# An S4 convolution beside a feed-forward block: where the first half's sums wait, and how the convolution's last step joins them

## The chip, the cores and the metric

The kernel runs on one core of one Trainium2 chip. Its time is the device time of one execution in microseconds (us), from the first to the last of the program's work. The runs before the change took 1136.37 us in the median of three (1135.81 to 1136.94).

Five engines of the core appear in the texts: PE (TensorE, the matrix multiplier), ACT (ScalarE), DVE (VectorE), POOL (GpSimd) and SP (SyncE, which here issues DMAs only). Each engine works through its own list of instructions in order. An instruction waits until the semaphores that it names allow it to go, and what stands behind it on the same engine waits with it. DMAs are issued by an instruction of SP, ACT or POOL and then run on the core's 16 DMA engines.

## What is computed

For 2048 tokens of width 576 the reference gives the sum of three terms: the input itself, a state-space convolution (S4, 128 states per channel, done by FFT) of the normalised input, and a feed-forward block with SiLU of the same normalised input.

```python
x = A_u                                   # (1, 2048, 576)
xn = _layernorm(x)
# _A_ref: K[d, l] = Re sum_n C dt B exp(dt A l);  y = irfft(rfft(xn) * rfft(K))[:L] + xn * Dskip
# _B_ref: silu(xn @ w1) @ w2,  w1 (576, 4608), w2 (4608, 576)
return x + _A_ref(xn, ...) + _B_ref(xn, w1, w2)
```

## The kernel before

All data is float32. For accuracy each matrix operand is split into a rounded part and a rest (`gh` and `gl`, `w1h` and `w1l`, the two planes of `w`), and a product is three matmuls of the parts. ACT makes the rounded part by a cast, DVE the rest by a subtraction.

**Tokens.** The 2048 tokens are 16 groups of 128, numbered j = 0 to 15; "token j" in the texts means such a group. Groups 0 to 7 are the first half, 8 to 15 the second. Each half is two blocks of four groups (b = 0, 1). An accumulator `acc[j]` of 128x576 in SBUF begins as x and takes up the feed-forward sum; two groups share one tile (`pairs`), and the pool `accp` has four such tiles, so the eight accumulators of one half fill it.

**Feed-forward.** `ffn` goes through the hidden width in chunks c of 4 x 128. For each (half, chunk, block) `up` multiplies by w1 (L289 to L291), applies SiLU on ACT (L297), and splits the result into `gh` (L298) and `gl` (L299); `down` multiplies by w2 into two PSUM banks `po` (L318) and DVE adds them to `acc[j]` (L323). The weights are loaded on SP into `w1r` (L244 to L246) and `w2r` (L266) and split (`w1h` on ACT L361, `w1l` on DVE L362 in the later part; `w` on ACT L275 and DVE L277). Split w2 tiles of the first half are kept in the scratch `dw2` and loaded again on POOL in the second (`w<-dw`, L471). From the third chunk of the second half on, `wino_ffn` does the products with w1 in a form with seven instead of eight block products (L444, L450, with sums of quarters on DVE, L372 to L375, and combinations `f`, L519).

**Between the halves.** At the first half's last chunk, when group j is complete, `down` stores `acc[j]` to a scratch in device memory, `dr0` (L326, on SP, shown as `dr<-acc`). After an odd j it loads x for groups 7+j and 8+j into a new tile of `accp` (L328 calls `load_x`, whose four DMAs are at L166, on SP).

**Convolution.** `side` is a second generator that `weave` steps through at positions (0 to 1) between the steps of `ffn`. It normalises x, transposes it (`spread`, L139 to L158, with loads `xr` on SP, stores `d1u<-u` on POOL), builds the kernel's spectrum (`kgen`, DVE and ACT work at L776 to L883), multiplies spectra (`spectral`, L889 to L942) and leaves d2 in device memory (`d<-yo`). What is left is the last step: a multiplication by a small matrix `s4`, by `conv` (L1005), with 64x32 tiles of the matrix multiplier, eight matmuls per group into two PSUM banks. Its operands `ys` are loaded on SP by `conv_load` (L993, two DMAs of 288 KB per group, six groups ahead).

**Tail.** `tail`, the last part of `side`, does that step for groups 0 to 7. `load_r0` loads two stored sums from `dr0` (L953, one DMA of 576 KB on SP, shown as `r<-dr`); `last` does `conv` for one group into two banks of the pool `pss` and DVE adds these to the loaded sums (`add_conv`, L1016); after the second group of a pair `store` writes the pair to the output with four DMAs on POOL (L173, `out_dram<-r`). The positions are in `tail_at`. For groups 8 to 15 the step is done in `down` at the second half's last chunk: `conv` writes two groups into four banks (`begun`; L1005, shown as `po`), and the feed-forward matmuls add to the same banks.

PSUM has eight banks in three pools: `ps1` (2 banks: `ph`, `pa`, `pc`), `ps2` (3 banks: `po`, `pb`) and `pss` (3 banks, used by `side`). The pair that `begun` holds lies in ps2 (first group) and ps1 (second group).

**Order.** The order of the instructions on each engine is not that of the program text: a scheduler that simulates the timeline places them, led by priorities (`tc.high_priority`) and by pinned dependences (`behind`).

Of the kernel before, what the change touches and what calls it, by code (L numbers as in the profile page):

```python
# [10 lines left out]
F32 = mybir.dt.float32  # L11
F32R = mybir.dt.float32r
AF = mybir.ActivationFunctionType
ALU = mybir.AluOpType
# [3 lines left out]
P = 128  # L18
L = 2048
D = 576  # L20
# [4 lines left out]
HD = D // 2  # L25
# [16 lines left out]
def kernel(  # L42
# [21 lines left out]
    nc = tc.nc  # L64
# [13 lines left out]
    dram = ctx.enter_context(tc.tile_pool(name="dram", bufs=1, space=DRAM))  # L78
# [2 lines left out]
    d2 = dram.tile([32 * P, D], F32, name="d2")  # L81
    dxt = [dram.tile([P, 9, 512], F32, name=f"dxt{b}") for b in range(2)]
    dxn = dram.tile([P, NJ, D], F32, name="dxn")
    dr0 = dram.tile([8 * P, D], F32, name="dr0")
    dw2 = dram.tile([NFT - WINO_C * FT, P, 2, D], F32, name="dw2")
    dexp = dram.tile([P, 4 * D], F32, name="dexp")

# [15 lines left out]
    accp = ctx.enter_context(tc.tile_pool(name="accp", bufs=4))  # L103
# [3 lines left out]
    ps1 = ctx.enter_context(tc.tile_pool(name="ps1", bufs=2, space=PSUM))  # L107
    ps2 = ctx.enter_context(tc.tile_pool(name="ps2", bufs=3, space=PSUM))
    pss = ctx.enter_context(tc.tile_pool(name="pss", bufs=3, space=PSUM))

    acc = {}
# [20 lines left out]
    pairs = {}  # L132
# [29 lines left out]
    def load_x(j, pool, tag, engines):  # L162

        t = pool.tile([P, 2, D], F32, tag=tag, name=f"{tag}{j}")
        for ps, v, eng in quarters(xv, engines):
            eng.dma_start(t[ps], v[:, j:j + 2])  # L166
        pairs[j] = t
        return t[:, 0, :], t[:, 1, :]

    def store(t, j, engines):  # L170

        for ps, v, eng in quarters(ov, engines):
            eng.dma_start(v[:, j:j + 2] if len(t.shape) > 2 else v[:, j], t[ps])  # L173

    def norm(p0, js, xs):

# [52 lines left out]
    def ffn():  # L229
# [71 lines left out]
        def down(blk, jj, terms=None):  # L301
            half, c, b = blk
            j = 8 * half + 4 * b + jj
            js = slice(jj * P, (jj + 1) * P)
            if half == 1 and c == NCH - 1 and jj % 2 == 0:
                for i, (pool, tag) in enumerate(((ps2, "ps2"), (ps1, "ps1"))):
                    begun[j + i] = [pool.tile([P, 512], F32, tag=tag, name="po") for _ in range(2)]
                conv((j, j + 1), (begun[j], begun[j + 1]))
                for i in range(2):
                    conv_load(j + i + AHEAD)  # L310
            terms = terms or [(G[blk, t], W2[half, c, t]) for t in range(FT)]
            for h in range(2):
                hs = slice(h * HD, (h + 1) * HD)
                po = begun[j][h] if j in begun else ps2.tile([P, 512], F32, tag="ps2", name="po")
                n = 0
                for gs, ws in terms:
                    for g, w in ((0, 0), (0, 1), (1, 0)):
                        pins["pe"] = nc.tensor.matmul(po[:, :HD], gs[g][:, js], ws[:, w, hs],  # L318
                                                      start=n == 0 and j not in begun, stop=n == 3 * len(terms) - 1,
                                                      skip_group_check=j in begun).ins  # L320
                        n += 1
                with tc.high_priority():
                    nc.vector.tensor_add(acc[j][:, hs], po[:, :HD], acc[j][:, hs])  # L323
            if half == 0 and c == NCH - 1:
                rows = slice(j * P, (j + 1) * P)
                nc.sync.dma_start(dr0[rows, :], acc[j])  # L326
                if j % 2:
                    acc[7 + j], acc[8 + j] = load_x(7 + j, accp, "acc", (nc.sync,))  # L328

        def next_xt(b):  # L330
            xt = new_xt(2 + b)
# [614 lines left out]

    def tail():

        r0s = {}

        def load_r0(j):
            r0s[j] = yp.tile([P, 2, D], F32, tag="r0", name="r0", bufs=2)
            nc.sync.dma_start(r0s[j], dr0[j * P:(j + 2) * P, :].rearrange("(i p) d -> p i d", p=P))  # L953

        def last(j):
            add_conv(j, r0s[j - j % 2][:, j % 2, :])
            conv_load(j + AHEAD)
            if j % 2:
                store(r0s[j - 1], j - 1, (nc.gpsimd,))

        steps, at = [], tail_at[0]
        for j in range(8):
            for f in (conv_load, load_r0)[j >= AHEAD:2 - j % 2]:
                steps.append((at, f, j))
                at += tail_at[1]
        steps += [(tail_at[2] + j * tail_at[3], last, j) for j in range(8)]
        for at, f, j in sorted(steps, key=lambda v: v[0]):
            yield at
            with behind(pins["load"]):
                f(j)  # L970
# [18 lines left out]
    def conv_load(j):  # L989
        if j < NJ:  # L990
            yss[j] = yp.tile([P, 4, HD], F32, tag="ys", name="ys", bufs=AHEAD)
            for h in range(2):
                nc.sync.dma_start(yss[j][64 * h:64 * h + 64],  # L993
                                  d2[j * 256:(j + 1) * 256, h * HD:(h + 1) * HD].rearrange("(q r) d -> r q d", q=4))

    def conv(js, banks):

        ys = [yss.pop(j) for j in js]
        first = pins["pe"]
        for n in range(8 * len(js)):  # L1000
            i, q1, q2, h = n // 8, n // 4 % 2, n // 2 % 2, 1 - n % 2
            o = 64 * q1 + 32 * q2
            rows = slice(64 * h, 64 * h + 64)
            with tc.high_priority() if n else nullcontext(), behind(first):
                mm = nc.tensor.matmul(banks[i][h][o:o + 32, :HD], s4[rows], ys[i][rows, 2 * q2 + q1],  # L1005
                                      start=True, stop=True, tile_position=(64 * h, o), skip_group_check=True)
            if n == 0:
                first = mm.ins

    def add_conv(j, dst):  # L1010

        py = [pss.tile([P, 512], F32, tag="pss", name="py") for _ in range(2)]
        conv((j,), (py,))
        for h in range(2):
            hs = slice(h * HD, (h + 1) * HD)
            nc.vector.tensor_add(dst[:, hs], py[h][:, :HD], dst[:, hs])  # L1016

    def gate_of(i):

        return (FT + i * 2 * FT + 1) / (2 * NCH * 2 * 2 * FT)  # L1020
# [1 line left out]
    def side():  # L1022
        nonlocal s4, kl, yp, pa, kfp, tail_at
        marks = (0.1357, 0.613, 0.855)
        tail_at = (0.893, 0.003, 0.930, 0.005)
        with tc.tile_pool(name="pa", bufs=4) as pa:
            for js in ((0, 1), (2, 3), (4, 5), (6, 7)):
                with behind(pins["xt3"] if js[0] > 2 else None):
                    phase0(pa, js)
                pins[f"xt{js[1]}"], pins[f"xt{js[1]}s"] = pins["xt_v"], pins["xt_s"]  # L1030
                if js[0] == 2:
                    yield 0
            yield 0
        with tc.tile_pool(name="kf", bufs=1) as kfp:
            for n in ("f", "rho", "phi"):
                kf[n] = kfp.tile([P, D], F32, name=n + "T")
            with tc.tile_pool(name="nat", bufs=1) as nat, tc.tile_pool(name="pb", bufs=2) as pb:
                nt = natural(nat)
                tiles = iter(range(8, NJ, 2))
                for at, tables in ((0.0, 1), (0.02, 0), (0.035, 0), (gate_of(1), 1), (0.06, 0), (gate_of(2), 1), (0.08, 0), (0.085, 1)):  # L1040
                    yield at
                    if tables:
                        next(nt, None)
                    else:
                        j = next(tiles)
                        with behind(pins["gl"]):
                            phase0(pb, (j, j + 1))
            with behind(pins["sd"]):
                nc.gpsimd.dma_start(f1, cf1)
            nc.sync.dma_start(vt, cv)  # L1050
            with tc.tile_pool(name="up", bufs=1) as up:
                sp = spread(up)
                for n, at in enumerate(kgen()):
                    if n > 1:
                        next(sp, None)
                    yield marks[0] + at * (marks[1] - marks[0])
                for _ in sp:
                    pass
        s4p = ctx.enter_context(tc.tile_pool(name="s4p", bufs=1))
        s4 = s4p.tile([P, 32], F32, name="s4")  # L1060
        nc.gpsimd.dma_start(s4, cs4)

        xp = ctx.enter_context(tc.tile_pool(name="xp", bufs=1))
        with tc.tile_pool(name="sx", bufs=1) as sx:
            for k, _ in enumerate(wino_x(sx, xp)):
                yield (171 + k) / 276
        with tc.tile_pool(name="kl", bufs=1) as kl:
            for at in spectral():
                yield 176 / 276 + (at - 1) * (marks[2] - 176 / 276)
        yp = ctx.enter_context(tc.tile_pool(name="yp", bufs=3))  # L1070
        yield from tail()
# [89 lines left out]
```

## Time and profile before

| | |
|---|---|
| median of three runs | 1136.37 us (1135.81 to 1136.94) |
| the profiled execution | 1141.59 us |
| its span (first to last instruction) | 1139.8 us |
| mean granted clock of PE | 0.990 |
| busy: PE, DVE, ACT, POOL | 1104.0, 955.5, 721.1, 113.4 us |
| moved by DMA | 176.04 MB, mean 154 GB/s |

The profile shows one execution. Times are in us from the start of the span unless marked ns. A timeline row gives the start, the duration, engine, line of the kernel's text, operation, destination<-source, the tile shape, and the count of equal instructions put together; in brackets the idle time before it and what released the engine. PE's float32 matmuls appear as several records each. "SPq" rows are the issuing of DMAs by SP; their duration includes waiting between the DMAs of one group, and the time to landing is told elsewhere. A row of the waits gives the waiting engine and line, what it waited for, the sum, the count and the longest. The table of stretches gives, for each stretch of time, the busy time and count for each engine, the granted clock of PE (PEclk, 1.00 is full), the busy share of the DMA engines and their rate.

### The profile page before, as it was taken

Reading aid. Unit: us, or ns where it says so; the run is one execution under the profiler, and the core shown is the slowest. Engines: PE = TensorE matmul, PEld = TensorE weight load, DVE = VectorE, ACT = ScalarE, POOL = GpSimd, SP = SyncE. Lnnn points to the kernel's source line nnn. Section 1 sums busy time; section 2 is a strip of 40 time slices with the busy share of each in tenths; the row PEclk is TensorE's granted clock in tenths of the full one; section 3 lists DMA queues with packets and bytes.
Section 4 is the critical chain, followed back from the end, with each engine's and each line's share of the span. In section 5 each row is a group of like instructions: output and inputs, shape, how many; then the busy total and the mean of one; then the engine's idle time right before and its main releaser. Section 6 shows DMA issues by size and latency. Waiting matters only on the chain.

```text
span 1139.8 us, 23099 instructions
## 1 busy us (share of the span) xinstructions
PE 1104.0 (97%) x9101; PEld 991.5 (87%) x9101; DVE 955.5 (84%) x1631; ACT 721.1 (63%) x1269; POOL 113.4 (10%) x206
## 2 busy tenths in 40 slices
PE   6999999999999999999989999999999999999798
PEld 5998989888988899899988889999989899998576
DVE  6698898999999999999979988988888888884432
ACT  4665456676677666676747646887867777772210
POOL 1001000000000000000000002112112112210111
PEclk9999999999999999999989999999999999999899
DMA  9456523536263625376844137556455556547964
GB/s 274 131 160 197 165 97 101 144 109 167 83 166 108 188 86 150 109 218 215 230 124 115 54 64 219 153 172 181 141 161 148 171 171 187 176 121 180 260 172 109
DMA packets 171405, 176.04 MB, mean 154 GB/s; under 512 B 88432, under 2 KB 136576, under 8 KB 170656
## 3 DMA queue, kind: packets, MB, share of 16 engines
q1 hardware_dynamic: 150128, 120.91, 38.4%
q0 software_dynamic: 20784, 52.76, 14.7%
q8 instruction: 72, 1.18, 0.4%
q10 hardware_dynamic: 384, 0.89, 0.3%
q14 instruction: 37, 0.30, 0.1%
HBM read 112.00 MB, written 62.60 MB: 153 GB/s over the span
## 4 chain that ended last, share of the span: by engine, by line
PE 52%; DVE 21%; DMA 10%; issue 7%; ACT 7%; SPq 1%; POOL 1%; DVEq 0%; ACTq 0%; POOLq 0%
PE po L318 23%; PE ph L289 12%; DMA w1r<-in_B_w_dram 5%; PE pb L444 3%; DVE acc L323 2%; PE kp L855 2%; PE pc L444 2%; DMA w2r<-in_B_w_dram 1%; DVE th L798 1%; DMA ys<-d 1%; DVE S L834 1%; DVE C L834 1%; PE pb L986 1%; PE pu L986 1%; DVE gl L299 1%
## 5 line engine op out<-in xcount | busy, mean ns | idle before, releaser
L318 PE MATMUL po<-w,gh 128*128 128x288 f32 x2304 | 479.5, 297 | 8.2 <-ACT gh L298 3.8
L318 PEld LDWEIGHTS po<-w,gh 128*128 128x128 f32 x2304 | 378.2, 189 | 26.7 <-issue 5.6
L318 PE MATMUL po<-w,gl 128*128 128x288 f32 x1152 | 337.3, 297 | 0.4 <-DVE gl L299 0.4
L318 PEld LDWEIGHTS po<-w,gl 128*128 128x128 f32 x1152 | 216.2, 189 | 3.9 <-issue 1.4
L323 DVE TENSOR_TENSOR acc<-po,acc 128x288 f32<-128x288 f32 x296 | 130.5, 451 | 61.9 <-PE po L318 60.6
L289 PE MATMUL ph<-xh,w1h 128*128 128x512 f32 (+1 forms) x368 | 99.7, 389 | 0.9 <-ACT xh L124 0.6
L289 PE MATMUL ph<-xl,w1h 128*128 128x512 f32 (+1 forms) x368 | 99.3, 387 | 0.0
L289 PE MATMUL ph<-xh,w1l 128*128 128x512 f32 (+1 forms) x368 | 98.1, 383 | 0.0
L297 ACT ACTIVATE gf<-ph 128x512 f32<-128x512 f32 (+1 forms) x92 | 53.1, 577 | 48.8 <-PE ph L291 36.0
L289 PEld LDWEIGHTS ph<-xl,w1h 128*128 128x128 f32 x368 | 67.7, 192 | 12.9
L289 PEld LDWEIGHTS ph<-xh,w1l 128*128 128x128 f32 x368 | 66.8, 190 | 12.0
L289 PEld LDWEIGHTS ph<-xh,w1h 128*128 128x128 f32 x368 | 65.5, 192 | 11.3 <-ACT xh L124 0.9
L814 ACT ACTIVATE c<-th,magic 128x1040 f32<-128x1040 f32 x36 | 42.0, 1168 | 39.8 <-DVE C L835 31.6
L158 POOL DMA_DIRECT2D d1u<-u x32 | 17.3, 542 | 460.2 <-ACT u L157 460.2
L299 DVE TENSOR_TENSOR gl<-gf,gh 128x512 fp32r<-128x512 f32 (+1 forms) x92 | 60.6, 660 | 2.9 <-ACT gh L298 2.7
L298 ACT CAST gh<-gf 128x512 fp32r<-128x512 f32 (+1 forms) x92 | 55.2, 601 | 10.2 <-PE po L318 9.0
L816 ACT ACTIVATE c<-th 128x1040 f32<-128x1040 f32 x36 | 38.7, 1074 | 31.1 <-DVE th L815 31.1
L361 ACT CAST w1h<-w1r 128x512 fp32r<-128x512 f32 (+2 forms) x56 | 34.5, 619 | 37.1 <-DMA w1r<-in_B_w_dram 36.0
L892 POOL DMA_DIRECT2D m<-in_cm_dram x64 | 34.5, 539 | 223.7 <-PE pu L986 140.3
L362 DVE TENSOR_TENSOR w1l<-w1r,w1h 128x512 fp32r<-128x512 f32 (+2 forms) x56 | 38.3, 685 | 21.7 <-ACT w1h L361 21.7
L834 DVE TENSOR_TENSOR S<-th,C 128x1024 f32<-128x1024 f32 x36 | 43.9, 1219 | 9.8 <-ACT th L817 9.7
L461 DVE TENSOR_TENSOR gl<-gf,gh 128x512 fp32r<-128x512 f32 x56 | 37.8, 687 | 10.8 <-ACT gh L460 10.5
(268 smaller groups left out, 2372.2 us busy)
## 6 DMA issues: line engine op xcount, KB each, us to landing
w1r<-in_B_w_dram SPq DMA_DIRECT2D x35, 512.0 KB, 4.2
dw<-w SPq DMA_DIRECT2D x28, 576.0 KB, 4.7
w<-dw POOLq DMA_DIRECT2D x28, 576.0 KB, 5.8
w2r<-in_B_w_dram SPq DMA_DIRECT2D x44, 288.0 KB, 5.0
d1u<-u POOLq DMA_DIRECT2D x32, 288.0 KB, 2.7
d1k<-stage SPq DMA_DIRECT2D x18, 512.0 KB, 7.0
ur<-d1u SPq DMA_DIRECT2D x32, 288.0 KB, 4.0
kr<-d1k SPq DMA_DIRECT2D x32, 288.0 KB, 3.0
```

What stands on the lines that cost most here:

```text
L289: nc.tensor.matmul(ph, w[:, kt, :], v[:, kt, a:e], start=n + kt == 0, stop=False)
L297: nc.scalar.activation(gf, ph, AF.Silu)
L298: pins["gh"] = nc.scalar.copy(gh, gf).ins
L299: pins["gl"] = nc.vector.tensor_sub(gl, gf, gh).ins
L318: pins["pe"] = nc.tensor.matmul(po[:, :HD], gs[g][:, js], ws[:, w, hs], start=n == 0 and j not in begun, stop=n == 3 * len(terms) - 1, ski ...
L323: nc.vector.tensor_add(acc[j][:, hs], po[:, :HD], acc[j][:, hs])
L362: nc.vector.tensor_sub(l[:, :k], src, h[:, :k])
L444: pins["pe"] = nc.tensor.matmul(dst, a[:, kt], v[:, kt], start=start and n == 0, stop=stop and n == 5, skip_group_check=True).ins
L461: pins["gl"] = nc.vector.tensor_sub(gl, gf, gh).ins
L814: nc.scalar.activation(c65, th, AF.Identity, bias=magic)
L816: nc.scalar.activation(c65, th, AF.Abs)
L834: nc.vector.tensor_mul(ov3, t[:, :, 0:64].rearrange("n d (x y) -> n d x y", y=32), mv3)
```

## The change

The scratch `dr0` goes, with its stores, its loads (`load_r0`) and the additions of `add_conv`. When the second group of a pair of the first half is complete, `down` stores the pair's sums straight to the output, with four DMAs on POOL; the loads of x for the second half's accumulators move from SP to POOL. In the tail, `last` does `conv` for two groups at once into four PSUM banks (one of ps2, three of pss), ACT copies them to a tile `yt`, and four DMAs on POOL with an accumulating operation add that tile to the output in device memory. The position of `last` goes from 0.930 to 0.932. For groups 8 to 15 the banks of a pair alternate: one of ps2 and three of pss for the first pair of a block, two of ps2 and two of ps1 for the second, where all pairs had ps2 and ps1 before.

```diff
--- before.py
+++ after.py
@@ -81,7 +81,6 @@
     d2 = dram.tile([32 * P, D], F32, name="d2")
     dxt = [dram.tile([P, 9, 512], F32, name=f"dxt{b}") for b in range(2)]
     dxn = dram.tile([P, NJ, D], F32, name="dxn")
-    dr0 = dram.tile([8 * P, D], F32, name="dr0")
     dw2 = dram.tile([NFT - WINO_C * FT, P, 2, D], F32, name="dw2")
     dexp = dram.tile([P, 4 * D], F32, name="dexp")
 
@@ -167,10 +166,10 @@
         pairs[j] = t
         return t[:, 0, :], t[:, 1, :]
 
-    def store(t, j, engines):
+    def store(t, j, engines, **more):
 
         for ps, v, eng in quarters(ov, engines):
-            eng.dma_start(v[:, j:j + 2] if len(t.shape) > 2 else v[:, j], t[ps])
+            eng.dma_start(v[:, j:j + 2] if len(t.shape) > 2 else v[:, j], t[ps], **more)
 
     def norm(p0, js, xs):
 
@@ -303,8 +302,9 @@
             j = 8 * half + 4 * b + jj
             js = slice(jj * P, (jj + 1) * P)
             if half == 1 and c == NCH - 1 and jj % 2 == 0:
-                for i, (pool, tag) in enumerate(((ps2, "ps2"), (ps1, "ps1"))):
-                    begun[j + i] = [pool.tile([P, 512], F32, tag=tag, name="po") for _ in range(2)]
+                pools = (((ps2, "ps2"), (pss, "pss")), ((pss, "pss"),) * 2) if jj == 0 else (((ps2, "ps2"),) * 2, ((ps1, "ps1"),) * 2)
+                for i in range(2):
+                    begun[j + i] = [pool.tile([P, 512], F32, tag=tag, name="po") for pool, tag in pools[i]]
                 conv((j, j + 1), (begun[j], begun[j + 1]))
                 for i in range(2):
                     conv_load(j + i + AHEAD)
@@ -322,10 +322,9 @@
                 with tc.high_priority():
                     nc.vector.tensor_add(acc[j][:, hs], po[:, :HD], acc[j][:, hs])
             if half == 0 and c == NCH - 1:
-                rows = slice(j * P, (j + 1) * P)
-                nc.sync.dma_start(dr0[rows, :], acc[j])
                 if j % 2:
-                    acc[7 + j], acc[8 + j] = load_x(7 + j, accp, "acc", (nc.sync,))
+                    store(pairs[j - 1], j - 1, (nc.gpsimd,))
+                    acc[7 + j], acc[8 + j] = load_x(7 + j, accp, "acc", (nc.gpsimd,))
 
         def next_xt(b):
             xt = new_xt(2 + b)
@@ -946,24 +945,19 @@
 
     def tail():
 
-        r0s = {}
-
-        def load_r0(j):
-            r0s[j] = yp.tile([P, 2, D], F32, tag="r0", name="r0", bufs=2)
-            nc.sync.dma_start(r0s[j], dr0[j * P:(j + 2) * P, :].rearrange("(i p) d -> p i d", p=P))
-
         def last(j):
-            add_conv(j, r0s[j - j % 2][:, j % 2, :])
-            conv_load(j + AHEAD)
-            if j % 2:
-                store(r0s[j - 1], j - 1, (nc.gpsimd,))
-
-        steps, at = [], tail_at[0]
-        for j in range(8):
-            for f in (conv_load, load_r0)[j >= AHEAD:2 - j % 2]:
-                steps.append((at, f, j))
-                at += tail_at[1]
-        steps += [(tail_at[2] + j * tail_at[3], last, j) for j in range(8)]
+            y = yp.tile([P, 2, D], F32, tag="yt", name="yt", bufs=2)
+            py = [[pool.tile([P, 512], F32, tag=tag, name="py") for pool, tag in pools]
+                  for pools in (((ps2, "ps2"), (pss, "pss")), ((pss, "pss"),) * 2)]
+            conv((j, j + 1), py)
+            for i in range(2):
+                for h in range(2):
+                    nc.scalar.copy(y[:, i, h * HD:(h + 1) * HD], py[i][h][:, :HD])
+                conv_load(j + i + AHEAD)
+            store(y, j, (nc.gpsimd,), accum_op=ALU.add)
+
+        steps = [(tail_at[0] + j * tail_at[1], conv_load, j) for j in range(AHEAD)]
+        steps += [(tail_at[2] + j * tail_at[3], last, j) for j in range(0, 8, 2)]
         for at, f, j in sorted(steps, key=lambda v: v[0]):
             yield at
             with behind(pins["load"]):
@@ -1007,14 +1001,6 @@
             if n == 0:
                 first = mm.ins
 
-    def add_conv(j, dst):
-
-        py = [pss.tile([P, 512], F32, tag="pss", name="py") for _ in range(2)]
-        conv((j,), (py,))
-        for h in range(2):
-            hs = slice(h * HD, (h + 1) * HD)
-            nc.vector.tensor_add(dst[:, hs], py[h][:, :HD], dst[:, hs])
-
     def gate_of(i):
 
         return (FT + i * 2 * FT + 1) / (2 * NCH * 2 * 2 * FT)
@@ -1022,7 +1008,7 @@
     def side():
         nonlocal s4, kl, yp, pa, kfp, tail_at
         marks = (0.1357, 0.613, 0.855)
-        tail_at = (0.893, 0.003, 0.930, 0.005)
+        tail_at = (0.893, 0.003, 0.932, 0.005)
         with tc.tile_pool(name="pa", bufs=4) as pa:
             for js in ((0, 1), (2, 3), (4, 5), (6, 7)):
                 with behind(pins["xt3"] if js[0] > 2 else None):
```

## What was predicted

> **What bounds the kernel now.** I read the page's busy times first, then a table of stretches of time, then the engine timelines around the stretches where TensorE stood still.
>
> ```profile
> PE 1104.0 (97%) x9101; PEld 991.5 (87%) x9101; DVE 955.5 (84%) x1631; ACT 721.1 (63%) x1269; POOL 113.4 (10%) x206
> core 0: us, PE busy (x) PEld busy (x) DVE busy (x) ACT busy (x) POOL busy (x), PEclk, DMA share, GB/s
> 570.00:580.00 10.00, 7.00 (x46) 5.76 (x44) 5.01 (x7) 3.04 (x5) 0.00 (x0) 0.94 0.78 236
> 580.00:590.00 10.00, 9.72 (x44) 9.15 (x45) 9.94 (x16) 4.97 (x10) 0.54 (x1) 0.72 0.29 83
> 1055.00:1060.00 5.00, 4.42 (x43) 3.64 (x41) 0.00 (x0) 0.00 (x0) 1.96 (x4) 1.00 1.09 233
> 1060.00:1065.00 5.00, 0.00 (x0) 0.00 (x0) 0.00 (x0) 0.00 (x0) 0.00 (x0) 0.85 1.08 300
> 1065.00:1070.00 5.00, 2.47 (x6) 1.99 (x7) 3.65 (x9) 1.14 (x2) 0.00 (x0) 0.50 1.09 231
> ```
>
> TensorE (PE) is busy 97% of the span, so work taken from another engine is worth nothing by itself; only what makes PE idle or adds to its own work counts. The stretches show two places where PE stands still and where its granted clock falls behind it (0.72 and 0.50): at 577 and at 1060. The change touches the queues at both, and it also touches PE work of the tail. I take the three in turn.
>
> **The stall at 577: the stores of the first half.** Lines of PE, ACT and SP, in that order:
>
> ```profile
> 576.44 0.42 PE L318 MATMUL po<-w,gh 128*128 128x288 f32 x2
> 576.70 0.30 PE L318 MATMUL po<-w,gl 128*128 128x288 f32 x1
> 580.28 1.33 PE L318 MATMUL po<-w,gh 128*128 128x288 f32 x4 [3.28 <-ACT gh L298]
> 582.36 0.68 PE L318 MATMUL po<-w,gh 128*128 128x288 f32 x2
> 582.84 0.44 PE L318 MATMUL po<-w,gl 128*128 128x288 f32 x1
> 585.24 0.63 PE L318 MATMUL po<-w,gh 128*128 128x288 f32 x2
> 578.41 0.67 ACT L275 CAST w<-w2r 128x576 fp32r<-128x576 f32 x1 [6.93 <-DMA w2r<-in_B_w_dram]
> 568.85 3.07 SPq L166 DMA_DIRECT2D acc<-in_A_u_dram  x4
> 572.97 0.40 SPq L326 DMA_DIRECT2D dr<-acc  x1
> 573.41 0.99 SPq L266 DMA_DIRECT2D w2r<-in_B_w_dram  x2
> SPq L166 <- DMA dr<-acc: 13.7, 4, 4.4
> 568.62 0.75 DVE L277 TENSOR_TENSOR w<-w2r,w 128x576 fp32r<-128x576 f32 x1
> ```
>
> PE waits 3.28 us for gh. Its ScalarE (ACT) cast stands on ACT behind the cast of a w2 tile, which waited 6.93 us for the load of w2r. That load was issued at 573.41 and used at 578.41, 5.00 us later. It could not be issued earlier because SP works in order: ahead of it stood four loads of acc from 568.85, which waited for the stores of the half's sums to the scratch dr (4 waits, 13.7 us in the stretch from 520 to 600, the longest 4.4), and more such stores up to 572.97. The load's buffer itself was free when VectorE (DVE) ended L277, at 568.62 + 0.75 = 569.37.
>
> In the changed kernel both these stores and these loads stand on POOL. The order in which its SP instructions are built has nothing but w1r, xr and w2r there. So w2r goes out at 569.4 and can be used at 569.4 + 5.0 = 574.4. In the trace gh was there 580.28 − 578.41 = 1.87 us after the cast of w2r began, so it comes at 576.3, before PE asks for it at 577.0. The 3.28 us go, and with them the slow matmuls behind: spacing is (576.70 − 576.44) / 2 = 0.13 us before the stall and (582.84 − 582.36) / 2 = 0.24 after it, until 585.24. That is 585.24 − 580.28 = 4.96 us, of which 4.96 × (1 − 0.13/0.24) = 2.3 is loss. Together 5.5. The slack is 0.7 us only, and landings vary, so I take **5.0**; the ends are 2 (the load lands 2 us later than assumed, with a shorter stall and its slow clock left) and 5.6. What is late next is nothing that I can see up to 590.
>
> What POOL gets is 4 stores per pair and 4 loads per pair, 32 in all. Queued behind them there are the stores of the transposed u and the loads of the next half's xt. POOL is free in that stretch (0.00 us busy from 570 to 580), so I cost this at nothing. The cover is that idle time; if the loads of acc, waiting on POOL for the stores to land as they did on SP, hold the u stores by 4.4 us, those have the wait of the next spread step to use up.
>
> **The stall at 1060: the loads of r0.** SP, then DVE, a link of the chain of waits, and PE:
>
> ```profile
> 1035.35 0.60 SPq L953 DMA_DIRECT2D r<-dr  x1
> 1039.49 0.62 SPq L953 DMA_DIRECT2D r<-dr  x1
> 1040.16 10.35 SPq L993 DMA_DIRECT2D ys<-d  x6
> 1055.07 0.49 SPq L246 DMA_DIRECT2D w1r<-in_B_w_dram  x1
> 1055.07 10.61 DMA w1r<-in_B_w_dram
> 1041.54 0.69 DVE L362 TENSOR_TENSOR w1l<-w1r,w1h 128x512 fp32r<-128x512 f32 x1
> 1068.46 0.45 DVE L323 TENSOR_TENSOR acc<-po,acc 128x288 f32<-128x288 f32 x1
> 1068.12 0.42 DVE L372 TENSOR_TENSOR w1r<-w1r 128x256 f32<-128x256 f32 x1
> 1067.53 0.79 PE L450 MATMUL pb<-x,w1h 128*128 128x512 f32 x1 [8.11 <-DVE f L519]
> ```
>
> PE waits 8.11 us for f, which stands on DVE behind the split of a w1 tile. The last part of that tile's load was issued at 1055.07 and landed at 1055.07 + 10.61 = 1065.68, though its buffer was free at 1041.54 + 0.69 = 1042.2. SP had ys loads and two r0 loads of 576 KB ahead of it, and the DMA engines were full (share 1.09, 233 GB/s from 1055 to 1060). Without r0, 2 × 576 KB / 233 GB/s = 4.9 us of transfer are gone: the load lands at about 1060.8. The ys loads stay ahead of it, so the stall does not vanish. In the built order of DVE, one acc addition and two quarter sums (0.45 and 0.42 us) come between the split and f, together 1.3 us, of which overlapping starts leave about 1.1. So PE resumes 4.9 − 1.1 = **3.8** us sooner. The ends are 2 (the accumulating stores of tokens 0 to 3, which read and write, take the bandwidth that r0 left) and 7 (no such traffic, and the sums fit into DVE's waits). The granted clock of 0.50 after the stall I leave as it is, since a stall of about 4 us remains and 3.28 us was enough at 577. The page "TensorE: Matmul & The Clock Gate" of the Trainium skill, Part 1, puts the gate at about 3.4 us of idling; the 3.28 us at 577 lie just under that and slow matmuls followed all the same, so the trace speaks for the lower figure here. By the page, a stall cut below 3.4 us would spare a loss like the 2.3 us worked out for 577, and the sum would be so much larger.
>
> **The convolution's runs on PE.** A stretch of PE in the tail, two pieces of the chain, and the tile's row (count, least, median and greatest ns):
>
> ```profile
> 1053.08 0.29 PE L318 MATMUL po<-w,gl 128*128 128x288 f32 x1
> 1053.31 0.71 PE L1005 MATMUL py<-ys,s 64*32 64x288 f32 x16
> 1053.95 0.72 PE L444 MATMUL pb<-xh,w1h 128*128 128x512 f32 x2
> 1054.52 0.63 PE L444 MATMUL pb<-xl,w1h 128*128 128x512 f32 x2
> 1073.42 0.65 PE py L1005 x16
> 1076.81 0.62 PE py L1005 x8
> L1005 PE MATMUL py<-ys,s x128: 402/415/427, 1044.1 to 1098.1; 64*32 64x288 f32 x128
> ```
>
> From the last po to the pb behind the run are 0.87 us instead of 0.13, and that pb takes 0.09 longer than the next: a run of 16 records (one token, two records per matmul) costs 0.83 us. In the chain a run of 8 (half a token) is only 0.03 us shorter: 0.80. So the price is mostly that of entering and leaving the small tiles, and it is paid per run. Before there are 10 runs of 16 and 12 of 8: 8.3 + 9.6 = 17.9 us. The built order of the changed kernel has 11 runs: 3 of half a token, 8 of 12 or 16 matmuls. No row has a run of two tokens. From below: another token adds as little as the second half does, 0.03 to 0.06, giving 0.9. From above: it costs as much as a whole run, 1.66. A run of 16 spans 0.71 us with records of 0.415, so its starts spread over 0.30 in two steps; a second token adds two more, about 0.5, and I take 1.34. Sum: 3 × 0.80 + 8 × 1.34 = 13.1, a gain of **4.8** (8.3 to 2.2).
>
> **What the tail gets in exchange.**
>
> ```profile
> 582.56 0.41 ACT L157 COPY u<-pu 128x288 f32<-128x288 f32 x1
> L886 POOL DMA_DIRECT2D d1k<-in_A_Dskip_dram x1: 858/858/858, 671.8 to 671.8; - x1
> DMA to landing us min/median/max: 3.7/3.7/3.7
> L173 POOL DMA_DIRECT2D out_dram<-r x16: 489/490/513, 1055.2 to 1101.1; - x16
> PE po L318 <- DMA w<-dw: 0.6, 1, 0.6
> ```
>
> Sixteen ACT copies of 128x288 at 0.41 us replace DVE additions; ACT was idle for most of this stretch. They cost only where they stand ahead of a cast that PE waits for: the built order has one such place, five copies, then gh, gh, w1h; I put three copies on the path there, 1.2 us. The pair also takes one of three ps2 banks that the down projection rotates through: 0.3. Sixteen accumulating stores stand on POOL for sixteen plain ones (the nearest row issues one in 0.86 us against 0.49): 4 × 0.37 = 1.5 us later for the loads of w from dw behind such a batch, of which the built order has two groups. PE waited once, for 0.6 us, for such a load in the tail, so no long lead covers it: between 0 and 3.0, and I take 0.5, since the batch is mostly issued before the loads' buffers come free. Together **−2.0**, between +0.5 (DVE freed of its additions) and −5.7 (three copies more on the path, 1.2, and the whole 3.0). The tail's end, the last po sums and their stores, is untouched.
>
> **Sum.** 5.0 + 3.8 + 4.8 − 2.0 = 11.6 us. The profiled execution takes 1141.59 us, of which its span is 1139.8, so 1130.0 in its own terms; it lies 5.2 over the median of the runs, and that lies as far below: 1136.37 − 11.6 = 1124.8.
>
> **The rivals.** (1) The middle gains nothing: moved transfers are moved, not saved. For it: the same bytes go between 545 and 590, and the acc loads wait for the same landings. Against it: w2r waited unissued behind waiting instructions while POOL was idle, and its 5.00 us from issue to use were short against 10.6 in the full tail. Time: 3.8 + 4.8 − 2.0 = 6.6, so 1129.8. The Trainium skill's page "DMA: Bandwidth & Descriptors", section "Issuing engines are not separate DMA queues", says that all queues share the same 16 engines, so that issuing elsewhere saves the issuing time alone, not transfer time; the order of SP's rows above is what speaks against its use here. (2) The tail's gain is eaten: two tokens per run do not overlap (gain 2.2), the stall shortens by 2, copies cost 4. Then 5.0 + 2 + 2.2 − 4 = 5.2: 1131.2. (3) Slower: accumulating stores hold POOL. If one occupies the queue until it lands, 3.7 us by the row of L886 instead of 0.86, a pair holds it 4 × 3.7 = 14.8 us. Two groups of w loads stand behind such a batch of 4; each comes 4 × (3.7 − 0.86) = 11.4 us later, 22.8 us of PE waits if nothing covers them, less the 11.6: slower by 11.2, 1147.6. It turns at 8 × (t − 0.86) = 11.6, t = 2.3 us of queue per store. The trace has one accumulating DMA, and it took 0.86; that speaks against it. (4) The runs stay as short as before because the scheduler splits the pairs: the built order, 11 for 22, excludes it.
>
> **How the numbers follow.** The forecast has 0.62; (1) 0.14, (2) 0.10, (3) 0.14. A measurement of this kernel can tell about 0.2%, 2.3 us. Faster: 0.62 + 0.14 + most of (2), 0.83; same 0.03; slower 0.14. With every term at its good end the gain is 5.6 + 7 + 8.3 + 0.5 = 21.4 (1115.0), at its bad end 2 + 2 + 2.2 − 5.7 = 0.5 (1135.9). I take 1115 to 1135, which holds (1) and (2) and leaves out (3) and the case that every bad end comes at once.
>
> **What would show it.** Right: PE's line at 577 without a wait for gh, and clock 1.0 in 580:590; w2r issued near 569.4; the wait for f at 4 to 5 us, w1r landed near 1061; 11 conv runs, a pair near 1.3 us. Wrong: acc loads on POOL ahead of u stores that PE's pu then waits for; PE waiting for w<-dw after a batch of accumulating stores (rival 3); PE waiting for gh or w1h behind yt copies.

## The result and the profile after

The changed kernel takes 1130.61 us in the median of four runs (1130.41 to 1131.51), the kernel before 1136.65 beside it; the ratio is 0.9957, 95% interval 0.9937 to 0.9976. It is faster by 6.0 us where 11.6 was forecast. The profiled execution took 1131.51 us with a span of 1129.7. That span is 10.1 us shorter than the one of before, more than the runs say, since the execution shown of before was a long one: on a second chip 17 runs of the kernel before lay between 1134.24 and 1141.61.

The page, the waits of PE (sum, count, longest), and stretches around the two stalls of before:

```profile
PE 1096.6 (97%) x9101; PEld 991.0 (88%) x9101; DVE 948.9 (84%) x1615; ACT 725.8 (64%) x1285; POOL 134.4 (12%) x238
PE po L318 <- DVE acc L323: 9.3, 3, 8.1
PE pu L154 <- ACT stage L877: 2.3, 1, 2.3
550.00:560.00 10.00, 7.71 (x28) 5.92 (x27) 7.90 (x14) 6.14 (x10) 2.52 (x5) 0.83 0.83 163
570.00:580.00 10.00, 10.00 (x180) 8.54 (x178) 9.86 (x15) 8.48 (x14) 4.35 (x10) 1.00 0.76 222
580.00:590.00 10.00, 10.00 (x62) 9.08 (x60) 9.00 (x16) 4.01 (x7) 0.77 (x2) 1.00 0.26 83
1055.00:1060.00 5.00, 3.60 (x14) 3.50 (x15) 4.47 (x10) 1.02 (x2) 0.00 (x0) 0.50 0.48 102
```

The stall at 577 is gone, with its slow clock: 10.00 of 10 us and a clock of 1.00 on both sides of 580. In its place stands a new wait at 550 with a clock of 0.83. The long stall of the tail is still 8.1 us, at 1048 now, and its releaser is no longer `f` but an addition to acc.

**The new wait at 550.** PE, ACT, SP and POOL of the changed kernel:

```profile
552.82 0.40 PE L154 MATMUL pu<-sp,s 128*128 128x288 f32 x1 [2.29 <-ACT stage L877]
551.54 0.72 ACT L256 CAST w1h<-w1r 128x640 fp32r<-128x640 f32 x1 [6.49 <-DMA w1r<-in_B_w_dram]
540.53 0.59 SPq L245 DMA_DIRECT2D w1r<-in_B_w_dram  x1
529.95 1.96 POOL L172 DMA_DIRECT2D out_dram<-acc  x4 [3.17 <-DVE acc L323]
534.99 0.55 POOL L332 DMA_DIRECT2D xl<-dxt  x1 [2.50 <-DMA out_dram<-acc]
535.62 1.96 POOL L165 DMA_DIRECT2D acc<-in_A_u_dram  x4
537.57 0.58 POOL L331 DMA_DIRECT2D xh<-dxt  x1
```

PE's `pu` waits for an ACT copy that stands behind the cast of a w1 tile, and that tile's load was used 551.54 − 540.53 = 11.0 us after its issue. On POOL the pair's four stores went out at 529.95, and the load of xl came after a wait of 2.50 us. The profile puts this wait down to the stores, but the kernel with the later loads of acc (below) has the same 2.50 us behind PE's `ph`, so it is probably not theirs. The loads of acc followed between xl and xh. So the loads of xl, acc (the x of the second half) and xh all went out within 3.2 us, just ahead of w1r on SP.

In the kernel before, ACT used the same tile 549.52 − 541.65 = 7.9 us after its load was issued, and PE did not stop there:

```profile
549.52 1.36 ACT L257 CAST w1h<-w1r 128x640 fp32r<-128x640 f32 x2 [3.34 <-DMA w1r<-in_B_w_dram]
```

**The stall at 1048.** PE, SP, a link of the chain, and DVE:

```profile
1056.40 0.85 PE L318 MATMUL po<-w,gh 128*128 128x288 f32 x2 [8.12 <-DVE acc L323]
1026.42 10.53 SPq L987 DMA_DIRECT2D ys<-d  x12
1041.93 12.85 DMA w1r<-in_B_w_dram
1055.42 0.56 DVE L361 TENSOR_TENSOR w1l<-w1r,w1h 128x384 fp32r<-128x384 f32 x1 [13.55 <-ACT w1h L360]
1055.90 0.45 DVE L323 TENSOR_TENSOR acc<-po,acc 128x288 f32<-128x288 f32 x1
```

Both kernels are compared from their first ys load, at 1034.03 before and 1026.42 after. Counted from there, the w1r load landed at 1065.68 − 1034.03 = 31.65 us in the kernel before and at 1054.78 − 1026.42 = 28.36 in the changed one: 3.3 sooner. PE resumed at 1067.53 − 1034.03 = 33.50 us before and at 29.98 after: 3.5 sooner, near the 3.8 of the forecast. But PE began to wait at 25.39 before (1059.42) and at 21.86 after (1048.28), also 3.5 sooner, so that the wait is as long as it was. In the built order of DVE the addition that frees a `po` bank now stands behind the split of w1r (1055.42, then 1055.90); in the kernel before, two such additions (at 1051.82 and 1053.41) went ahead of that split. So PE stopped for the bank before it had done the work that it did ahead of the stall before: 264 records of the down projection (L318) were still to come after the stall in the kernel before, 288 in the changed one. The 24 more, at 0.13 us each, are 3.2 of the 3.5 us.

**The convolution's runs.** PE around one run of two tokens:

```profile
1065.16 0.29 PE L318 MATMUL po<-w,gl 128*128 128x288 f32 x1
1065.38 1.23 PE L999 MATMUL py<-ys,s 64*32 64x288 f32 x32
1066.54 0.53 PE L318 MATMUL po<-w,gh 128*128 128x288 f32 x2
1068.10 0.29 PE L318 MATMUL po<-w,gl 128*128 128x288 f32 x1
1068.32 0.69 PE L999 MATMUL py<-ys,s 64*32 64x288 f32 x8
1068.94 0.53 PE L318 MATMUL po<-w,gh 128*128 128x288 f32 x2
```

From po to po 1.38 us, less 0.13, plus 0.11 for a first pair of matmuls of 0.53 in place of 0.42: 1.36 for 32 records (1.34 was forecast), and by the same working 0.82 for 8 (0.80 was). With 3 short and 8 long runs that is 13.3 us for 17.9, a gain of 4.6.

### The profile page after: what moved, and what is told of

Its sections match the earlier page's. It is cut to its first block, busy times and chain, and to the rows that moved or that the text cites. A ratio compares the mean times of both kernels' runs of the same rounds, so it can differ in the third digit from the quotient of the medians.

```text
span 1129.7 us, 23101 instructions
## 1 busy us (share of the span) xinstructions
PE 1096.6 (97%) x9101; PEld 991.0 (88%) x9101; DVE 948.9 (84%) x1615; ACT 725.8 (64%) x1285; POOL 134.4 (12%) x238
## 4 chain that ended last, share of the span: by engine, by line
PE 72%; DVE 11%; DMA 8%; ACT 3%; issue 3%; SPq 1%; POOL 0%; DVEq 0%; ACTq 0%; POOLq 0%
PE po L318 31%; PE ph L288 16%; PE pb L443 5%; DMA w1r<-in_B_w_dram 4%; PE pc L443 3%; PE kp L854 3%; PE pu L980 2%; PE pk L980 2%; PE pb L980 2%; PE ph L289 1%; PE ph L290 1%; DVE acc L323 1%; PE z L869 1%; DMA w2r<-in_B_w_dram 1%; PE pa L443 1%
## 5 line engine op out<-in xcount | busy, mean ns | idle before, releaser
L318 PE MATMUL po<-w,gh 128*128 128x288 f32 x2304 | 477.5, 297 | 11.8 <-DVE acc L323 9.3
L318 PEld LDWEIGHTS po<-w,gh 128*128 128x128 f32 x2304 | 377.1, 188 | 28.4 <-DVE acc L323 10.5
L318 PE MATMUL po<-w,gl 128*128 128x288 f32 x1152 | 336.7, 296 | 0.6 <-DVE gl L298 0.6
L318 PEld LDWEIGHTS po<-w,gl 128*128 128x128 f32 x1152 | 215.9, 188 | 2.7 <-DVE gl L298 0.9
L971 ACT CAST yh<-ka 128x576 fp32r<-128x576 f32 x32 | 21.7, 677 | 38.7 <-DVE ka L917 38.6
```

## The experiments

Twelve experiments ran on three chips, four on each, with runs of the kernel before on each chip: medians 1138.11, 1138.89 and 1137.81. A difference between kernels of different chips is therefore taken by their ratios to before. An edit can also change the order that the scheduler builds elsewhere: the number of the convolution's runs is 11 in the changed kernel, but 9 in some of the kernels below, and this is said there. By the prices above, 9 runs (one short, eight long) in place of 11 are worth about 1.6 us.

**The kernel before, once more** (no edit).

> The kernel before, unchanged, for a second profiled execution. The first one took 1141.59 us where the median of the runs is 1136.65. If that surplus of 5 us lies in stalls that come and go with the landing of loads, this execution is near 1136.5 and one of the waits at 577 (3.28 us) or 832 (2.0 us) is shorter or gone; if the surplus is spread evenly or lies outside the stalls, both waits stand as before.

It took 1139.76 us. The wait at 577 (3.7 us) and the one at 832 (2.7 us) stand as before, and so does the stall of the tail, so they are not accidents of the first execution:

```profile
PE pb L450 <- DVE f L519: 8.5, 1, 8.5
PE po L318 <- ACT gh L298: 4.1, 2, 3.7
```

Where the first execution's surplus lies is not settled by this.

**The middle alone.**

```diff
-                nc.sync.dma_start(dr0[rows, :], acc[j])
                 if j % 2:
-                    acc[7 + j], acc[8 + j] = load_x(7 + j, accp, "acc", (nc.sync,))
+                    for i in (j - 1, j):
+                        nc.gpsimd.dma_start(dr0[i * P:(i + 1) * P, :], acc[i])
+                    acc[7 + j], acc[8 + j] = load_x(7 + j, accp, "acc", (nc.gpsimd,))
```

> The kernel before with only the queue of the first half's stores (still to the scratch dr0) and of the following loads of x moved from SP to POOL. Theory: the wait for gh at 577 goes (3.28 us and 2.3 us of slow clock), and a wait of some 2.3 us behind a late w1r load near 550 takes its place, as in the trace after: a net gain of 0 to 2 us, 1134.5 to 1136.5. Rival (the forecast's own term): 5 us, 1131.5.

1134.68 us for 1138.11, ratio 0.9971 (0.9956 to 0.9985): 3.4 us, between the two expectations. ACT and POOL:

```profile
569.76 0.67 ACT L275 CAST w<-w2r 128x576 fp32r<-128x576 f32 x1 [0.30 <-DMA w2r<-in_B_w_dram]
523.09 0.55 POOL L327 DMA_DIRECT2D dr<-acc  x1 [16.25 <-DVE acc L323]
531.20 1.97 POOL L166 DMA_DIRECT2D acc<-in_A_u_dram  x4 [0.83 <-issue]
533.29 0.58 POOL L333 DMA_DIRECT2D xl<-dxt  x1
```

ACT waits 0.30 us for w2r where it waited 6.93, as forecast, and PE's waits list none for `pu` at 550. Here the first store of the pair went at 523.09, so acc was loaded ahead of xl and not between xl and xh.

**The tail alone.**

```diff
-                    store(pairs[j - 1], j - 1, (nc.gpsimd,))
-                    acc[7 + j], acc[8 + j] = load_x(7 + j, accp, "acc", (nc.gpsimd,))
+                    store(pairs[j - 1], j - 1, (nc.sync,))
+                    acc[7 + j], acc[8 + j] = load_x(7 + j, accp, "acc", (nc.sync,))
```

> The changed kernel with the first half's stores and the loads of x put back on SP; the tail as changed. Theory: the tail alone brings nearly the whole measured gain, 4 to 6 us (the shorter convolution runs; the stall of 8 us stays): 1130.5 to 1132.5. Rival (the forecast's terms): 3.8 + 4.8 - 2.0 = 6.6 us, and the middle as much again, so the changed kernel should then stand 5 us below this one.

1128.07 us for 1138.11, ratio 0.9919 (0.9894 to 0.9944), more than either expectation and more than the changed kernel's own ratio (0.9943, below). So moving these DMAs to POOL brought the changed kernel nothing; it may have cost it, which the touching intervals leave open. The two kernels differ in the tail too, though, since the built order here has 9 runs of the convolution, and the wait of 8.1 us is replaced by one of 4.3 us. With the pair's stores on SP the wait for gh at 577 is gone as well (the 0.5 us of its row are at 233, and stand in the changed kernel too): ACT still waits 3.48 us for w2r, half of before, and PE waits 0.46 us behind that. In the tail PE waits once behind the copies to `yt`:

```profile
PE po L318 <- ACT gh L297: 0.5, 1, 0.5
PE po L318 <- ACT yt L955: 4.3, 1, 4.3
```

That copy itself stood on ACT behind the cast of w1r (1050.67), which had waited 8.22 us for the late load: it is the same late load as at 1048.

**Two tokens' ys ahead of w1r.**

```diff
-        steps = [(tail_at[0] + j * tail_at[1], conv_load, j) for j in range(AHEAD)]
+        steps = [(tail_at[0] + j * tail_at[1] if j < 2 else 0.931, conv_load, j) for j in range(AHEAD)]
```

> The changed kernel with only two tokens' ys loads ahead of the last w1r load on SP in place of six; the other four follow it. Theory: the 8 us stall near 1048 is the wait for that load alone, which then goes out as soon as its buffer is free at about 1035 and lands by 1045: the stall goes with its slow clock, 8 to 11 us less than the changed kernel, 1120 to 1123, unless ys come late in its place. Rival (the stall is one of PSUM banks, since the pair holds one of three ps2 banks): PE still waits for the DVE addition, 3 us or more stay, 1125 to 1128.

1124.47 us for 1138.11, ratio 0.9882 (0.9853 to 0.991), and by the ratios some 7 us under the changed kernel: less than the theory's 8 to 11, and not the rival's, since the wait for the DVE addition is gone from the tail. The built order here has 9 runs of the convolution, so about 1.6 of the 7 us may be theirs. What is left among PE's waits:

```profile
PE pu L154 <- ACT stage L877: 3.8, 1, 3.8
PE po L318 <- DMA w<-dw: 3.1, 3, 2.6
```

The first is the wait at 550, here longer than in the changed kernel's own execution; the second is a new late load in the tail, of w from dw, which stands on POOL behind accumulating stores.

**The changed kernel, once more** (no edit).

> The changed kernel, unchanged, for more runs and a second profiled execution. In the first, a wait of 2.3 us near 550 (PE's pu, behind ACT, behind a w1r load landed 11 us after its issue) stood where the kernel before had none, and the wait at 1048 was 8.1 us. Theory: both belong to the change and come again, within 1.5 us. Rival: the first belongs to that execution and is absent here.

1132.68 us for 1138.89, ratio 0.9943 (0.9926 to 0.996): 6.2 us, as in the first measurement. Both waits are there again:

```profile
PE po L318 <- DVE acc L323: 9.1, 3, 8.1
PE pu L154 <- ACT stage L877: 3.1, 1, 3.1
```

**The accumulators' loads later.**

```diff
-                    store(pairs[j - 1], j - 1, (nc.gpsimd,))
-                    acc[7 + j], acc[8 + j] = load_x(7 + j, accp, "acc", (nc.gpsimd,))
+                    stored = store(pairs[j - 1], j - 1, (nc.gpsimd,))     # store now returns its last DMA
+                    for i in {1: (), 3: (), 5: (1, 3), 7: (5, 7)}[j]:
+                        with behind(stored):
+                            acc[7 + i], acc[8 + i] = load_x(7 + i, accp, "acc", (nc.gpsimd,))
```

> The changed kernel with the four loads of the second half's accumulators put behind later stores on POOL: none before the store of groups 4 and 5, so that none stands among the loads of the half's second xt near 535. Theory: the late w1r load of 550 is late because those 590 KB and the xt's 2.2 MB were issued in the same 3 us as it; without them it lands 2 us sooner or more, the wait near 550 falls under 0.5 us and the kernel gains 3 to 5 us on the changed one. Rival (the load is late because of the xt loads alone, or of the store at 544): the wait stays within 1 us and the time within 1.5 us.

1128.88 us beside the changed kernel's 1132.68 on the same chip: 3.8 us faster; ratio to before 0.9904 (0.9887 to 0.9922). SP's issue of the w1r load, ACT's use of it, and POOL:

```profile
539.27 0.60 SPq L246 DMA_DIRECT2D w1r<-in_B_w_dram  x1
546.38 1.36 ACT L257 CAST w1h<-w1r 128x640 fp32r<-128x640 f32 x2 [2.58 <-DMA w1r<-in_B_w_dram]
533.72 0.55 POOL L335 DMA_DIRECT2D xl<-dxt  x1 [2.50 <-PE ph L289]
534.63 0.55 POOL L334 DMA_DIRECT2D xh<-dxt  x1 [0.37 <-PE ph L289]
```

The load comes 7.1 us after its issue, not 11.0, and PE does not wait for `stage`. The loads of xl and xh are otherwise the same, so the loads of acc among them made w1r late. Whether they did it by their own bytes or by putting xh off, from 4.6 us ahead of w1r to 3.0, is not separated; nor is what the other loads of acc, which the edit moves too, have in the 3.8 us.

**One token per run.**

```diff
-            py = [[pool.tile([P, 512], F32, tag=tag, name="py") for pool, tag in pools]
-                  for pools in (((ps2, "ps2"), (pss, "pss")), ((pss, "pss"),) * 2)]
-            conv((j, j + 1), py)
             for i in range(2):
+                py = [pss.tile([P, 512], F32, tag="pss", name="py") for _ in range(2)]
+                conv((j + i,), (py,))
                 for h in range(2):
-                    nc.scalar.copy(y[:, i, h * HD:(h + 1) * HD], py[i][h][:, :HD])
+                    nc.scalar.copy(y[:, i, h * HD:(h + 1) * HD], py[h][:, :HD])
```

> The changed kernel with the last step of groups 0 to 7 done one group per run in two banks of pss, as before, so that ps2 keeps its three banks for po and pb; copies and accumulating stores as changed. Theory: PE reaches its wait for the last w1r load later, since it isn't held by a missing ps2 bank: the stall of 8 us falls by 2 to 4, the runs rise from 11 to 12 and are shorter, net 1 to 4 us faster than the changed kernel. Rival (the landing of w1r alone sets the time): the stall starts later but ends at the same work done, and the kernel is 0 to 2 us slower.

1130.55 us, 2.1 faster than the changed kernel; ratio to before 0.9924 (0.9909 to 0.994). SP, ACT, POOL, PE:

```profile
1027.45 10.55 SPq L986 DMA_DIRECT2D ys<-d  x12
1053.80 0.51 ACT L360 CAST w1h<-w1r 128x384 fp32r<-128x384 f32 x1 [11.76 <-DMA w1r<-in_B_w_dram]
1054.90 3.19 POOL L172 DMA_DIRECT2D out_dram<-yt  x4 [22.90 <-DVE w1l L361]
1056.24 0.85 PE L318 MATMUL po<-w,gh 128*128 128x288 f32 x2 [5.60 <-DVE acc L323]
```

The wait is 5.60 us for 8.12. It begins 23.19 us after the first ys (21.86 in the changed kernel), with 276 records of L318 still to come for 288. So the bank is worth some 1.3 us, as far as the other order of the convolution's runs (12 for 11) has no part in it. The wait ends at 28.79 for 29.98, 1.2 sooner; ACT used w1r 26.35 us after the first ys, for 1054.88 − 1026.42 = 28.46 in the changed kernel. The first accumulating stores went out after that landing here.

**Plain stores in place of the accumulating ones** (the addition for groups 0 to 7 is left out).

```diff
-            store(y, j, (nc.gpsimd,), accum_op=ALU.add)
+            store(y, j, (nc.gpsimd,))
```

> The changed kernel with plain stores in place of the four accumulating ones of each pair, which leaves the addition for groups 0 to 7 out. Theory: the accumulating form costs little, since nothing but two groups of w loads stands behind it: 0 to 1.5 us faster than the changed kernel, and POOL issues a store in about 0.5 us where the accumulating one takes 0.8. Rival (the accumulating stores read and write and so hold back w1r and ys): 3 us or more faster, with the wait at 1048 shorter by as much.

1130.15 us, 2.5 faster than the changed kernel, between the two expectations; ratio to before 0.9923 (0.9905 to 0.994), an interval that overlaps the changed kernel's. The rows of SP, ACT and PE, and of the store in this and then in the changed kernel (least, median, greatest ns):

```profile
1027.32 10.52 SPq L987 DMA_DIRECT2D ys<-d  x12
1053.62 1.14 ACT L360 CAST w1h<-w1r 128x384 fp32r<-128x384 f32 x2 [9.88 <-DMA w1r<-in_B_w_dram]
1055.15 0.85 PE L318 MATMUL po<-w,gh 128*128 128x288 f32 x2 [5.96 <-DVE acc L323]
L172 POOL DMA_DIRECT2D out_dram<-yt x16: 492/492/512, 1044.0 to 1091.3; - x16
L172 POOL DMA_DIRECT2D out_dram<-yt x16: 756/1090/1661, 1043.1 to 1092.5; - x16
```

w1r was used 26.30 us after the first ys, as with one token per run, where the changed kernel used it at 28.46 (28.43 in its second execution). Kernels in which no accumulating store is under way before the landing agree: 26.30, 26.35, and 26.60 in the tail alone, whose first accumulating store also came later. With such stores under way it was 28.84 with the later loads of acc and 27.61 with the banks of before (the last experiment but one). So those stores hold w1r back by 1 to 2.5 us, some 2.1 in the changed kernel.

**Both repairs**, the ys order and the later loads of acc (edits above).

> The changed kernel with both repairs: two tokens' ys ahead of the last w1r load on SP, and the accumulators' loads behind later stores on POOL. Theory (two separate late loads of w1r): the gains add, 3.8 us for the accumulators' loads and 8 for the ys order, so 11 to 13 us under the changed kernel, some 17 to 19 under the kernel before (ratio 0.984). Rival (what one repair frees is lost at the next late load, w from dw behind the accumulating stores, 2.6 us in the run with the ys order alone): 8 to 10 us under the changed kernel.

1119.8 us for 1137.81, ratio 0.9838 (0.9822 to 0.9854): 18.0 us under before, as the theory had it, though here too the built order has 9 runs of the convolution, which the theory did not count. The w1r load is used 4.4 us after its issue. SP, ACT, and PE's largest wait in the tail, with the stretch around it:

```profile
1033.30 0.60 SPq L246 DMA_DIRECT2D w1r<-in_B_w_dram  x1
1037.71 0.51 ACT L363 CAST w1h<-w1r 128x384 fp32r<-128x384 f32 x1 [2.83 <-DMA w1r<-in_B_w_dram]
1065.07 0.53 PE L319 MATMUL po<-w,gh 128*128 128x288 f32 x2 [2.65 <-DMA w<-dw]
1060.00:1070.00 10.00, 7.35 (x43) 6.37 (x42) 1.61 (x3) 1.22 (x3) 3.18 (x4) 1.00 1.11 294
```

**The accumulating stores held back one pair**, on top of both repairs.

```diff
-            store(y, j, (nc.gpsimd,), accum_op=ALU.add)
+            held.append((y, j))          # stored by a step 0.007 later
```

> As the kernel with both repairs, and the accumulating stores of a pair are issued one pair later, so that on POOL the loads of w from dw go ahead of them. Theory: PE's wait for w<-dw near 1068 (2.6 us with the ys order alone) goes, 2 to 3 us faster than with both repairs. Rival: the load is late because the DMA engines are full with ys, not for its place on POOL; no gain (within 1 us).

1116.99 us beside 1119.8, the ratios to before 0.9818 (0.9805 to 0.9832) and 0.9838, their intervals overlapping. It is the fastest kernel here. The largest wait for w from dw fell, but did not go:

```profile
1061.52 0.53 PE L319 MATMUL po<-w,gh 128*128 128x288 f32 x2 [1.81 <-DMA w<-dw]
```

That is 0.8 us of the 2.8, and another wait for w from dw grew from 0.4 to 1.0 us. So neither expectation is borne out in full, and where the rest of the 2.8 us comes from is not shown.

**The banks of before for groups 8 to 15.**

```diff
-                pools = (((ps2, "ps2"), (pss, "pss")), ((pss, "pss"),) * 2) if jj == 0 else (((ps2, "ps2"),) * 2, ((ps1, "ps1"),) * 2)
+                pools = ((ps2, "ps2"),) * 2, ((ps1, "ps1"),) * 2
```

> The changed kernel with the convolution of groups 8 to 15 in the banks of before (two of ps2, two of ps1 for each pair), which alone differs. The built order has 17 runs of small tiles in place of 11. Theory (a run of four or eight matmuls costs 0.8 us, one of 16 1.35): groups 8 to 15 take 11 runs at 0.8 = 8.9 us for 5 runs with 6.2 us: 2.5 to 3 us slower than the changed kernel. Rival (bank waits hidden by the alternation matter as well): 4 us slower or more.

1134.22 us for 1137.81, ratio 0.9968 (0.9956 to 0.998). Against the changed kernel's 0.9943 that is 2.8 us, as expected from 6 runs more; against its first ratio, 0.9957, 1.3. The intervals overlap, so the price of a run rests on the traces more than on this.

**The ys order in the kernel before.**

```diff
-                steps.append((at, f, j))
+                steps.append((at if j < 2 else 0.929 + 0.0001 * j, f, j))
```

> The kernel before with four ys loads and one r0 load ahead of the last w1r load in place of twelve and two. Theory: the stall of 8 us in the kernel before is likewise that load's place on SP: it shrinks by 5 us or more, 5 to 9 us faster than before, so that this gain needs nothing of the change. Rival: with the r0 and ys loads both to come, r0 or ys are late instead, and less than 3 us are gained.

1136.48 us for 1137.81, ratio 0.9992 (0.9977 to 1.0007): no gain that can be told. The rival holds. ACT, the chain, DVE and PE:

```profile
1044.64 0.51 ACT L361 CAST w1h<-w1r 128x384 fp32r<-128x384 f32 x1 [5.96 <-DMA w1r<-in_B_w_dram]
1059.36 12.28 DMA r<-dr
1071.77 0.46 DVE L1016 TENSOR_TENSOR r<-py,r 128x288 f32<-128x288 f32 x1 [9.83 <-DMA r<-dr]
1072.88 0.61 PE L318 MATMUL po<-w,gl 128*128 128x288 f32 x1 [6.90 <-DVE gl L461]
```

w1r is in time, but an r0 load then lands 12.28 us after its issue, DVE's addition of it waits 9.83 us, and behind that on DVE stands the `gl` that PE needs. The stall of 7 us has only moved. Without r0 (the changed kernel) the same order of ys takes it away.

## Why the prediction came out as it did

Two steps of the sum failed, and they carried 8.8 of its 11.6 us. One is the step that nothing else comes late when the DMAs move to POOL; the other takes the earlier landing of w1r as a gain, without asking when the stall begins.

- **The middle, 5.0 us.** The mechanism held: w2r went out unhindered (at 571.72, its buffer free at 571.70), the wait for gh and its slow clock are gone, and alone it is worth 3.4 us. What failed is the step "what is late next is nothing that I can see up to 590", and with it the cost of nothing for what POOL gets. The new wait lies ahead of the old one, at 550, where I had not looked. I had asked whether the waiting loads of acc hold the u stores; what they did was to slip between the loads of xl and xh and share the DMA engines with a w1r load. Putting the loads of acc later gives 3.8 us back, so that the term is about 0 in sum. The gh wait did not need POOL either: with one batch of stores per pair left on SP it was gone too, but for 0.46 us behind w.
- **Rival 1** (moved transfers are not saved) came near in size, for another reason than its own: the transfers cost more because they were moved in time. The rule of the page "DMA: Bandwidth & Descriptors" of the Trainium skill, "Issuing engines are not separate DMA queues", that all DMAs interleave on the same engines, agrees with these rows: 11.0 us to use of w1r among loads issued on POOL, 7.1 without those of acc.
- **The stall at 1060, 3.8 us.** The landing came 3.3 us sooner where 4.9 was worked out; the accumulating stores, which hold w1r back by 1 to 2.5 us by the runs, cover the 1.6 us between, and the lower end had named them. PE resumed 3.5 sooner. The step that failed is to take the 3.8 us by which PE resumes sooner as a gain, with the stall's start left where it was. The wait began 3.5 us sooner too, and work that had lain ahead of it now lies behind it, so that the stall is 8.12 us for 8.11 and the term is about 0. I had read in the built order of DVE that an acc addition stands behind the split, but counted only its 0.45 us on the way to f, and not that PE waits for the bank that it frees. A bank less in ps2, which I priced at 0.3, accounts for some 1.3 of the 3.5, by the run with one token per run.
- **The convolution's runs, 4.8 us.** Right: 11 runs, 1.36 and 0.82 us by the trace, 4.6 in sum. This is the only term of the gain that arrived whole, and most of the measured 6.0. What the other 1.4 us are is not shown.
- **The exchange, −2.0 us.** About the right size at the wrong place. PE waited for no load of w from dw in the changed kernel's tail (0.4 us in its second execution), so rival 3 is out, though an accumulating store held POOL for 1.09 us in the median, not 0.86. The price was paid in transfer time, some 2.5 us by the run with plain stores, and is contained in the stall above. The copies to `yt` held up nothing that PE waited for there.
- **Rival 2** (the tail's gain eaten, 1131.2) gave the time, but not by its mechanism: two tokens in one run do overlap.

## What to carry to other kernels

A load that is late because it stands behind others gives its time back only if nothing else is then late and if the engine that waits still has its work ahead of the wait: work out the start of the stall as well as its end. When transfers are moved to another queue, list what is issued in the same few microseconds there, and which load that someone waits for lands among it. Look for the order of the queue first: eight ys loads put behind one w1r load were worth about as much as the whole change (7 us, with 9 runs of the convolution in place of 11), though only once the r0 loads were gone.

## What the runs showed of the hardware

Whether an idle PE came back to a slow clock did not go by the length of the gap. After 2.29 us of idling at 550 the stretch of 10 us had a granted clock of 0.83, and after 3.28 us at 577 one of 0.72; after 2.65 us at 1062, in the kernel with both repairs, it had 1.00. So I was wrong to read 3.28 us as enough in general. Part 1 of the Trainium skill's page "TensorE: Matmul & The Clock Gate" tells of a window of about 3.4 us that runs free of the kernel, and of a slow clock after at least one idle window. That the length of the gap does not decide agrees with a free-running window; slow clocks behind gaps of 2.29 and 3.28 us do not agree with that length.

An accumulating store of 144 KB took POOL 0.76 to 1.66 us where the same store without accumulation took 0.49 to 0.51.
